# HGRN2 attention with a MetaFormer MLP on one core: chunk scores from a tree of levels, or as a quotient of scanned gate products

## The chip, the cores and the metric

The kernel runs on one core of a Trainium2 chip. That core has a matrix engine (TensorE, PE in the profile; its weight loads are PEld), three engines for elementwise work (VectorE or DVE, ScalarE or ACT, GpSimd or POOL), and a queue (SyncE or SP) from which all of this kernel's transfers are issued. Each engine works off its own instructions in order and waits on semaphores for the others. Matmuls write into PSUM, which the kernel uses in banks of 128 partitions by 512 fp32 numbers; everything else lies in SBUF. The metric is the device time of one execution in microseconds (us).

## The reference, cut to what matters

There are 4 batches, 8 heads, 768 tokens and 48 channels a head. Everything is fp32, except the two MLP weights, which come as float64.

```python
f = 1.0 / (1.0 + np.exp(-f_logit))                  # gates, per channel
for t in range(S):                                  # S = 768
    state = f[:, :, t, :, None] * state + np.einsum('bhd,bhe->bhde', k[:, :, t], v[:, :, t])
    y[:, :, t] = np.einsum('bhd,bhde->bhe', q[:, :, t], state)
x = y.transpose(0, 2, 1, 3).reshape(B, S, H * D)    # (4, 768, 384)
xn = (x - mean) / np.sqrt(var + 1e-06) * g_ln       # over the 384 channels
out = x + np.maximum(xn @ w_ch1, 0.0) @ w_ch2       # 384 -> 1536 -> 384
```

q, k and v are normal with spread 0.1, f_logit is normal with mean 2 and spread 0.5, so a gate is near 0.88. Written out, the weight of step s in step t is the product of the gates over (s, t], per channel. A chunk of tokens can therefore be done as matmuls: scores between the tokens of the chunk, times v, plus q (with the gates from the chunk's start) times the state that enters the chunk.

## The kernel before, in words

The work is cut into 12 units of 256 tokens of one batch (`units`, L71), three to a batch, as two chunks of 128 tokens. A unit has an attention part (`attention`, L180) and an MLP part (`mlp`, L320). Both are Python generators, and the order of all instructions is that in which the program issues them (`manual_schedule`): the loop at L366 to L379 runs, in turn, one step of the attention of unit n and one step of the MLP of unit n - 1. In round 0 the third partner is the conversion of w1 (`weights`, L129), in round 1 that of w2: each weight comes in six pieces of 768 numbers a partition, and each piece goes through DVE (L153), POOL (L155, L157), DVE (L159, L162), ACT (L164) and DVE (L165, L168), or, for w2, POOL at the end (L171).

Attention puts channels on partitions, two heads at partitions 0 and 64, by transposes through an identity on PE (tr, L192), from which ACT copies q and k (z, L198) and makes the gates by a sigmoid (L196). POOL multiplies gates up to products over blocks of 2 to 128 tokens (L207). The scores of a chunk are then made in levels. The diagonal comes first (pd, L218). Then, for blocks of 2, 4, up to 128 tokens, PE multiplies the first half's k with the second half's q (pl, L239), DVE multiplies q and k up to the next block size (L250) and copies the scores under a mask (L256; ACT at the last level, L253). Each level needs the one before. After seven levels k is transposed back (kp, L269), its product with v is the chunk's part of the state (pn, L292), and scores and carried state give y (py, L278 and L285). DVE advances the state (L301, L303), ACT copies y to x (L316).

The MLP normalizes x with DVE and POOL (L328 to L334), transposes it (xp, L341), and has 36 matmuls of 128 x 128 by 256 tokens (ph, L349) with a relu on ACT after each six (L351), then for each 128 tokens twelve accumulating matmuls by 384 columns (po, L356); DVE adds x (L361) and SP stores. ph, po, xp, tr and kp share four PSUM banks, one each; pd, pl and py share two buffers of two banks.

## Time and profile before

| | us |
|---|---|
| median of three runs (935.0, 940.1, 940.43) | 940.1 |
| the profiled execution: span, first to last instruction | 937.5 |
| PE busy | 811.8 (87%) |
| DVE busy | 367.9 (39%) |
| ACT busy | 136.7 (15%) |
| POOL busy | 86.6 (9%) |
| mean granted TensorE clock | 0.837 |

For the profiled execution nothing beside its span is known; the median lies 2.6 above it. The profile page gives, after busy times, the span in 40 equal slices of 23.4 us; a digit is the busy share in tenths. Then it has the chain of waits: followed back from the last instruction, at each step to what released it. A row of a group of instructions has the line, the engine, the operation, the tile written and the tiles read, the shapes, the count, the busy time, the mean of one in ns, and the idle time before it with what ended it. The granted clock is the share of full speed that PE was allowed. PE's records are pipelined, so the price of a group of matmuls is better read from start to start than from its duration.

### The profile page before, as it was taken

The page shows a single profiled execution, that of the slowest core. Times are in us where ns is not written, and L with a number is a line of the kernel's source. Part 1 is how long each engine was busy: PE and PEld are TensorE (multiplying, and loading weights), DVE is VectorE, ACT ScalarE, POOL GpSimd, SP SyncE. Part 2 cuts the span into 40 slices and gives each one's busy share as a digit, 9 for nine tenths or more (in the row PEclk, how much of TensorE's full clock was granted, in tenths as well). Part 3 has the DMA queues.
Part 4 walks back from the last instruction along what each step waited for, and adds up shares of the span by engine and source line. Part 5 has one row for each costly group of instructions (what it writes and reads, how often), then busy time and mean ns, then how long its engine had stood idle before and what let it go on. Part 6 is the DMA issues. An engine that isn't in the chain of part 4 may idle for free.

```text
span 937.5 us, 13603 instructions
## 1 busy us (share of the span) xinstructions
PE 811.8 (87%) x6056; PEld 651.6 (69%) x6056; DVE 367.9 (39%) x490; ACT 136.7 (15%) x229; POOL 86.6 (9%) x168
## 2 busy tenths in 40 slices
PE   3335567989989989989989989989989989989988
PEld 2335555758868768768768768768868868768765
DVE  1675377325225244135125235135225245245110
ACT  2011211111111111111111111111111111111110
POOL 4210333010010010010010010010010010010000
PEclk8555757897997988898897988897897998979989
DMA  9227120021050050050050050050050050000000
GB/s 190 79 67 135 34 68 34 1 57 29 1 84 2 1 85 1 1 85 1 1 85 1 1 84 1 1 85 1 2 80 5 1 84 1 1 17 1 10 8 17
DMA packets 106250, 33.91 MB, mean 36 GB/s; under 512 B 100816, under 2 KB 103888, under 8 KB 106192
## 3 DMA queue, kind: packets, MB, share of 16 engines
q1 hardware_dynamic: 106192, 33.04, 19.8%
q8 instruction: 48, 0.79, 0.3%
q14 instruction: 10, 0.08, 0.0%
HBM read 28.31 MB, written 4.72 MB: 35 GB/s over the span
## 4 chain that ended last, share of the span: by engine, by line
PE 76%; DVE 13%; ACT 4%; POOL 2%; SPq 2%; issue 1%; DMA 1%; POOLq 0%; ACTq 0%
PE ph L349 23%; PE po L356 21%; PE pl L239 18%; PE py L278 6%; DVE scores L221 3%; PE py L285 2%; DVE z L250 2%; PE xp L341 2%; SPq L89 2%; ACT z L198 2%; DVE scores L256 1%; PE pn L292 1%; DVE z L224 1%; PE pd L218 1%; PE kp L269 1%
## 5 line engine op out<-in xcount | busy, mean ns | idle before, releaser
L239 PE MATMUL pl<-z 48*128 48x64 f32 (+1 forms) x2688 | 204.8, 314 | 98.3 <-DVE z L224 59.9
L239 PEld LDWEIGHTS pl<-z 48*128 48x128 f32 (+1 forms) x2688 | 192.5, 226 | 125.1 <-issue 124.4
L349 PE MATMUL ph<-xt,w 128*128 128x256 f32 x864 | 237.3, 432 | 4.7 <-ACT xt L342 4.7
L349 PEld LDWEIGHTS ph<-xt,w 128*128 128x128 f32 x864 | 181.3, 217 | 37.9 <-ACT xt L342 5.3
L356 PE MATMUL po<-w,h 128*128 128x384 f32 x576 | 205.3, 513 | 0.0
L250 DVE TENSOR_TENSOR z<-z,gates 128x512 f32<-128x512 f32 x168 | 115.1, 727 | 165.0 <-PE pl L239 165.0
L356 PEld LDWEIGHTS po<-w,h 128*128 128x128 f32 x576 | 112.8, 201 | 73.4 <-issue 9.7
L256 DVE COPY_PREDICATED scores<-mask,pl 128x1024 f32<-128x1024 int32 x72 | 118.8, 1650 | 0.0
L207 POOL TENSOR_TENSOR gates<-gates 128x512 f32<-128x512 f32 (+6 forms) x84 | 36.0, 429 | 654.2 <-ACT gates L196 648.6
L351 ACT ACTIVATE h<-ph 128x512 f32<-128x512 f32 x72 | 42.9, 596 | 290.6 <-PE ph L349 290.6
L361 DVE TENSOR_TENSOR o<-x,po 128x384 f32<-128x384 f32 x24 | 13.3, 554 | 165.2 <-PE po L356 165.2
L301 DVE TENSOR_TENSOR state<-state,gates 128x192 f32<-128x192 f32 x16 | 5.7, 358 | 129.2 <-PE py L285 129.2
L278 PE MATMUL py<-v,scores 128*128 128x48 f32 x384 | 53.5, 300 | 0.0
L278 PEld LDWEIGHTS py<-v,scores 128*128 128x128 f32 x384 | 50.8, 214 | 1.1
L221 DVE COPY_PREDICATED scores<-diag,pd 128x512 f32<-128x512 int32 x48 | 30.4, 713 | 23.9 <-PE pd L218 23.9
L316 ACT COPY x<-py 128x768 f32<-128x768 f32 x12 | 9.6, 798 | 148.5 <-PE py L285 148.5
L218 PE MATMUL pd<-z 48*128 48x128 f32 x384 | 24.7, 278 | 5.3 <-ACT z L198 5.3
L196 ACT ACTIVATE gates<-tr 128x512 f32<-128x512 f32 x24 | 13.3, 596 | 106.2 <-PE tr L192 106.2
L218 PEld LDWEIGHTS pd<-z 48*128 48x128 f32 x384 | 22.4, 188 | 8.1 <-ACT z L198 7.9
L342 ACT COPY xt<-xp 128x384 f32<-128x384 f32 x24 | 11.4, 478 | 104.6 <-PE xp L341 104.6
L198 ACT COPY z<-tr 128x512 f32<-128x512 f32 x48 | 25.2, 616 | 2.7 <-PE tr L192 2.7
L285 PEld LDWEIGHTS py<-state,z 48*128 48x128 f32 x320 | 20.4, 195 | 7.4 <-issue 6.8
(55 smaller groups left out, 370.0 us busy)
## 6 DMA issues: line engine op xcount, KB each, us to landing
fraw<-in_f_logit_dram SPq DMA_DIRECT2D x24, 192.0 KB, 3.9
qraw<-in_q_dram SPq DMA_DIRECT2D x24, 192.0 KB, 4.8
kraw<-in_k_dram SPq DMA_DIRECT2D x24, 192.0 KB, 5.2
v<-in_v_dram SPq DMA_DIRECT2D x24, 192.0 KB, 4.9
w1words<-in_moe_w_ch_dram SPq DMA_DIRECT2D x6, 768.0 KB, 4.4
w2words<-in_moe_w_ch_dram SPq DMA_DIRECT2D x6, 768.0 KB, 4.3
out_dram<-o SPq DMA_DIRECT2D x24, 192.0 KB, 1.9
gain<-in_moe_g_ln_dram SPq DMA_DIRECT2D x1, 1.5 KB, 3.9
```

Of the source, the lines that this page charges most:

```text
L198: nc.scalar.copy(out=to, in_=pt)
L207: nc.gpsimd.tensor_tensor(out=prod[size], in0=pv[:, 0], in1=pv[:, 1], op=ALU.mult)
L218: nc.tensor.matmul(pd[:, par, a], lhsT=z[rows, 1, a, c * C:(c + 1) * C], rhs=z[rows, 0, a, c * C:(c + 1) * C], start=True, stop=True)
L221: nc.vector.copy_predicated(out=scv[:, par, c], mask=diag.unsqueeze(1).broadcast_to([P, NP, C]), data=pd[:, par])
L239: nc.tensor.matmul(plv[0:m, par, c, a].rearrange("s (n h) -> s n h", h=half), lhsT=z[rows, 1, a, c * C:c * C + m], rhs=late, start=True, s ...
L250: nc.vector.tensor_tensor(out=zz, in0=zz, op=ALU.mult, in1=pv[:, i].broadcast_to([P, nblk, half]))
L256: nc.vector.copy_predicated(out=sc.rearrange("s i (n two h) -> s two i n h", two=2, h=half)[:, 1], mask=masks[half].rearrange("s (o n h) - ...
L278: nc.tensor.matmul(py[:, par, at:at + D], lhsT=scv[:, par, c, a], rhs=vt[:, c, 2 * a + par], start=c == 0 and a == 0, stop=u == 0 and c == ...
L285: nc.tensor.matmul(py[:, par, at:at + D], lhsT=z[rows, 0, a, c * C:(c + 1) * C], rhs=state[rows, a], start=False, stop=True, skip_group_ch ...
L349: nc.tensor.matmul(ph[:, j], lhsT=w1[:, m, (i + j) * P:(i + j + 1) * P], rhs=xt[:, m], start=m == 0, stop=m == KD - 1)
L351: nc.scalar.activation(out=h[:, i:i + 2], in_=ph, func=AF.Relu)
L356: nc.tensor.matmul(po, lhsT=h[:, i, c * C:(c + 1) * C], rhs=w2[:, i], start=i == 0, stop=i == KF - 1)
```

## The change

Units are now 64 tokens of all four batches (256 tokens as before, 12 units), so that the chunk is 64 tokens and one unit follows another in every batch. The levels are gone. A scan on DVE multiplies the gates backward from each chunk's end (`after`, with a new start at every chunk by a zero in the gates), and k times it is kh. A second scan multiplies forward, started at one over the chunk's whole product (`upto`), and q times it is qh. Then kh times qh is the score in one matmul per batch and head, of which DVE keeps the lower triangle (`causal`). As the state that enters is multiplied by the whole product first (`kept`), qh serves for it too. POOL makes kh and qh. The padding channels of f are filled with 40, so that their gates are 1.

Scores, carried, values and state are four groups of 32 matmuls a unit with at most 64 rows and 64 weight columns, at four places of the array in turn. Transposes and MLP are as before in number and shape.

The order is written by slots: attention of units 0, 1 and 2 first, with w1's conversion (18 steps) cut in between; then for each m the MLP of unit m in 12 slots (six of ph, six of po), with the four stages of attention m + 3 behind slots 0, 1, 6 and 8, and normalization and transposes of unit m + 1 behind slots 9 and 10. During m = 0 three steps of w2's conversion, that is one whole piece, stand behind each slot until w2 is done. The weights of the next piece are fetched one piece ahead. w1's pieces are 256 columns of all three row blocks, so their last product is three instructions.

A quotient can overflow when the gates are small. So the least product of a chunk is kept (`least`), compared with 1e-12 near the end, and read into registers; if it is smaller, the kernel before, in a serial form (`general_path`), computes everything again behind a branch.

```diff
--- before.py
+++ after.py
...
+def general_path(tc, q, k, v, f_logit, w1, w2, ident, out):
...
+    for n in range(len(units)):
+        load(n)
+        for _ in attention(n):
+            pass
+        for _ in mlp(n):
+            pass
...
+    T = 64
+    G = B // 2
+    NP = H // 2
+    GA = G * NP
+    NS = 2 * GA
+    E1 = T + 1
...
+    AHEAD = 3
...
+    def load(n):
+        if n >= NU:
+            return
+        vt = raws.tile([P, G, H, D], FP32, tag="rawv", name=f"v{n}")
+        loaded[n] = [wide_heads[name, n % 2] for name in "fqk"] + [vt]
+        for t, src in zip(loaded[n], (f_logit, q, k, v), strict=True):
+            for b in range(B):
+                nc.sync.dma_start(
+                    out=t[(b % 2) * T:(b % 2 + 1) * T, b // 2, :, 0:D],
+                    in_=src[b, :, n * T:(n + 1) * T, :].rearrange("h p d -> p h d"))
...
+    ends = consts.tile([P, NS, E1], FP32)
+    nc.vector.memset(ends, 0.0)
+    nc.vector.memset(ends[:, :, T:E1], 1.0)
+    starts, gates = [], []
+    for i in range(2):
+        t = consts.tile([P, NS, E1], FP32, name=f"starts{i}")
+        nc.vector.memset(t, 0.0)
+        starts.append(t)
+        t = consts.tile([P, NS * E1 + 1], FP32, name=f"gates{i}")
+        nc.gpsimd.memset(t, 0.0)
+        gates.append(t)
+    least = consts.tile([P, NS], FP32)
...
+        r, w = (rows, PIECE // rows) if scaled else (PIECE // cols, cols)
...
+        fetch(0)
+        for i, (ci, fi) in enumerate(pieces):
+            if i + 1 < len(pieces):
+                fetch(i + 1)
...
+            nc.vector.tensor_scalar(out=scale, in0=high, scalar1=20, scalar2=0x7FF,
+                                    op0=ALU.logical_shift_right, op1=ALU.bitwise_and)
+            nc.gpsimd.tensor_scalar(out=scale, in0=scale, scalar1=float(BIAS + 255),
+                                    scalar2=float(BIAS), op0=ALU.min, op1=ALU.max)
+            nc.gpsimd.tensor_scalar(out=scale, in0=scale, scalar1=float(-BIAS),
+                                    scalar2=float(1 << 23), op0=ALU.add, op1=ALU.mult)
+            yield
+            nc.vector.scalar_tensor_tensor(out=scale, in0=high, scalar=-(1 << 31), in1=scale,
+                                           op0=ALU.bitwise_and, op1=ALU.bitwise_or)
+            nc.vector.tensor_scalar(out=high, in0=high, scalar1=0xFFFFF, scalar2=None,
+                                    op0=ALU.bitwise_and)
+            nc.scalar.activation(out=frac, in_=high, func=AF.Copy, bias=1.0, scale=2.0 ** -20)
+            yield
+            nc.vector.scalar_tensor_tensor(out=frac, in0=low, scalar=2.0 ** -52, in1=frac,
+                                           op0=ALU.mult, op1=ALU.add)
+            if scaled:
+                for c in range(r):
+                    nc.vector.scalar_tensor_tensor(
+                        out=to[:, c], in0=frac[:, c], scalar=gain[:, c:c + 1],
+                        in1=scale[:, c].bitcast(FP32), op0=ALU.mult, op1=ALU.mult)
...
+    def attention(n):
+        fr, qr, kr, vt = loaded.pop(n)
+        gt, st = gates[n % 2], starts[n % 2]
+        gv = gt[:, 0:NS * E1].rearrange("p (s e) -> p s e", e=E1)
...
+        for g in range(G):
+            pt = across(fr, g)
+            nc.scalar.activation(out=gv[:, g * 8:(g + 1) * 8, 1:E1], in_=pt, func=AF.Sigmoid)
...
+        after = work.tile([P, NS, E1], FP32, tag="after", bufs=2, name=f"after{n}")
+        nc.vector.tensor_tensor_scan(
+            out=after.rearrange("p s e -> p (s e)")[:, ::-1], data0=gt[:, NS * E1:0:-1],
+            data1=ends.rearrange("p s e -> p (s e)")[:, ::-1], initial=0.0,
+            op0=ALU.mult, op1=ALU.add)
+        total = work.tile([P, NS], FP32, tag="total", bufs=2, name=f"total{n}")
+        nc.vector.tensor_scalar_max(out=total, in0=after[:, :, 0], scalar1=1e-30)
+        nc.vector.reciprocal(out=st[:, :, 0], in_=total)
+        nc.vector.tensor_tensor(out=least, in0=least, in1=total, op=ALU.min)
+        upto = work.tile([P, NS, E1], FP32, tag="upto", name=f"upto{n}")
+        nc.vector.tensor_tensor_scan(
+            out=upto.rearrange("p s e -> p (s e)"), data0=gt[:, 0:NS * E1],
+            data1=st.rearrange("p s e -> p (s e)"), initial=0.0, op0=ALU.mult, op1=ALU.add)
+        yield
+        for src, dst in ((kr, zk), (qr, zq)):
+            for g in range(G):
+                pt = across(src, g)
+                nc.scalar.copy(out=dst[:, g * 8:(g + 1) * 8], in_=pt)
+        kh = work.tile([P, NS, T], FP32, tag="kh", bufs=2, name=f"kh{n}")
+        qh = work.tile([P, NS, T], FP32, tag="qh", bufs=2, name=f"qh{n}")
+        nc.gpsimd.tensor_tensor(out=kh, in0=zk, in1=after[:, :, 1:E1], op=ALU.mult)
+        nc.gpsimd.tensor_tensor(out=qh, in0=zq, in1=upto[:, :, 1:E1], op=ALU.mult)
+        yield
...
+        if n:
+            kept = work.tile([P, 2, GA, D], FP32, tag="kept", name=f"kept{n}")
+            nc.vector.tensor_tensor(
+                out=kept, in0=state, op=ALU.mult,
+                in1=total.rearrange("p (e b) -> p b e", b=2).unsqueeze(3).broadcast_to(
+                    [P, 2, GA, D]))
+        py = two_banks(f"py{n}")
+        if n:
+            for e, (g, a) in enumerate(pairs):
+                for b in range(2):
+                    for r in range(2):
+                        nc.tensor.matmul(py[half(b), r, e * D:(e + 1) * D],
+                                         lhsT=qh[head_rows(r), 2 * e + b],
+                                         rhs=kept[head_rows(r), b, e], start=e == 0, stop=False,
+                                         skip_group_check=True)
+        ps = two_banks(f"ps{n}").rearrange("s r (e t) -> s r e t", t=T)
+        for e, (g, a) in enumerate(pairs):
+            for b in range(2):
+                for r in range(2):
+                    seg = 2 * e + b
+                    nc.tensor.matmul(ps[half(b), r, e], lhsT=kh[head_rows(r), seg],
+                                     rhs=qh[head_rows(r), seg], start=True, stop=True)
+        sc = work.tile([P, 2, GA, T], FP32, tag="sc", name=f"sc{n}")
+        nc.vector.tensor_tensor(
+            out=sc.rearrange("s r e t -> s (r e) t"), in0=ps.rearrange("s r e t -> s (r e) t"),
+            in1=causal.unsqueeze(1).broadcast_to([P, 2 * GA, T]), op=ALU.mult)
+        kt = work.tile([P, GA, P], FP32, tag="kt", name=f"kt{n}")
+        for g in range(G):
+            pt = one_bank(f"kp{n}").rearrange("p (a c) -> p a c", a=NP)
+            for a in range(NP):
+                e = g * NP + a
+                nc.tensor.transpose(pt[:, a],
+                                    kh[:, 2 * e:2 * e + 2].rearrange("p b t -> p (b t)"), ident)
+            nc.scalar.copy(out=kt[:, g * NP:(g + 1) * NP], in_=pt)
+        yield
...
+        for across_ in range(2):
+            for e, (g, a) in enumerate(pairs):
+                for b in range(2):
+                    r = b ^ across_
+                    nc.tensor.matmul(py[half(b), r, e * D:(e + 1) * D],
+                                     lhsT=sc[half(b), r, e], rhs=vt[half(b), g, 2 * a + r],
+                                     start=n == 0 and e == 0, stop=True,
+                                     skip_group_check=True)
+        if n < NU - 1:
+            pn = two_banks(f"pn{n}")
+            for e, (g, a) in enumerate(pairs):
+                for r in range(2):
+                    for b in range(2):
+                        nc.tensor.matmul(pn[half(r), b, e * D:(e + 1) * D],
+                                         lhsT=kt[half(b), e, half(r)],
+                                         rhs=vt[half(b), g, 2 * a + r], start=True, stop=True)
+            pnv = pn[:, :, 0:GA * D].rearrange("p b (e d) -> p b e d", d=D)
+            if n:
+                nc.vector.tensor_tensor(out=state, in0=kept, in1=pnv, op=ALU.add)
+            else:
+                nc.vector.tensor_copy(out=state, in_=pnv)
+        x = xs.tile([P, G, DM], FP32, tag="x", name=f"x{n}")
+        x_of[n] = x
+        nc.scalar.copy(out=x.rearrange("t g (a r d) -> t r (g a) d", r=2, d=D),
+                       in_=py[:, :, 0:GA * D].rearrange("t r (e d) -> t r e d", d=D))
...
+        xn_of[n] = mv, rstd
+        yield
...
+    def normalize(n):
...
+    def turn(n):
...
+            for b in range(2):
+                nc.sync.dma_start(out=out[2 * g + b, n * T:(n + 1) * T, :], in_=o[half(b)])
...
+    load(1)
+    w1_parts = weights(w1, moe_w_ch1, "w1", True)
+    w2_parts = weights(w2, moe_w_ch2, "w2", False)
...
+    for n in range(AHEAD):
+        stages = attention(n)
+        next(stages)
+        some(w1_parts, 1)
+        next(stages)
+        load(n + 2)
+        some(w1_parts, 2)
+        next(stages)
+        some(w1_parts, 2)
+        next(stages)
+        some(w1_parts, 1)
+    some(w1_parts, 18)
+    normalize(0)
+    turn(0)
+    for m in range(NU):
+        n = m + AHEAD
+        stages = attention(n) if n < NU else iter(())
+        parts = mlp(m)
+        for slot in range(12):
+            next(parts)
+            if m == 0:
+                some(w2_parts, 3)
+            if slot == 0:
+                next(stages, None)
+            elif slot == 1:
+                next(stages, None)
+                load(n + 2)
+            elif slot == 6:
+                next(stages, None)
+            elif slot == 8:
+                next(stages, None)
+            elif slot == 9 and m + 1 < NU:
+                normalize(m + 1)
+            elif slot == 10 and m + 1 < NU:
+                turn(m + 1)
+            if m == NU - 2 and slot == 3:
...
+                nc.vector.tensor_scalar(out=small, in0=least_one, scalar1=LEAST, scalar2=None,
+                                        op0=ALU.is_lt)
+    fast.close()
+    too_small = nc.values_load(small[0:1, 0:1], min_val=0, max_val=1)
+    with tc.If(too_small > 0):
+        with tc.manual_schedule():
+            general_path(tc, q, k, v, f_logit, w1, w2, ident, out)
```

331 lines of the change are left out of this document (210 added, 121 removed).

## The prediction

> **What bounds the kernel now.** I read the page's busy times and slices first, then the chain of waits, then the timeline of one unit, then that of the start.
>
> ```profile
> span 937.5 us, 13603 instructions
> ...
> PE 811.8 (87%) x6056; PEld 651.6 (69%) x6056; DVE 367.9 (39%) x490; ACT 136.7 (15%) x229; POOL 86.6 (9%) x168
> ...
> PE   3335567989989989989989989989989989989988
> ...
> PE 76%; DVE 13%; ACT 4%; POOL 2%; SPq 2%; issue 1%; DMA 1%; POOLq 0%; ACTq 0%
> PE ph L349 23%; PE po L356 21%; PE pl L239 18%; PE py L278 6%; DVE scores L221 3%; PE py L285 2%; DVE z L250 2%; PE xp L341 2%; SPq L89 2%; ACT z L198 2%; DVE scores L256 1%; PE pn L292 1%; DVE z L224 1%; PE pd L218 1%; PE kp L269 1%
> ```
>
> TensorE holds 76% of the chain, and the MLP (ph and po) is only 44 points of it. The level matmuls (pl) are 18 points. So most of the span is PE-bound, except the first seven slices, where PE is 30 to 70% busy. The two must be costed apart. First one unit in the middle, PE alone; the columns are start, duration, engine, line, tile and records (an fp32 matmul leaves two records, a transpose one). The last column is idle time before.
>
> ```profile
> 488.71 3.48 PE L239 MATMUL pl<-z 48*128 48x64 f32 x32 [2.95 <-DVE z L224]
> ...
> 497.28 5.47 PE L349 MATMUL ph<-xt,w 128*128 128x256 f32 x12
> 502.68 2.00 PE L239 MATMUL pl<-z 48*128 48x64 f32 x32
> 504.62 2.86 PE L349 MATMUL ph<-xt,w 128*128 128x256 f32 x12
> 507.40 2.00 PE L239 MATMUL pl<-z 48*128 48x64 f32 x32
> ...
> 525.33 1.04 PE L269 MATMUL kp<-ident,z 128*128 128x128 f32 x8
> 526.21 2.75 PE L356 MATMUL po<-w,h 128*128 128x384 f32 x8
> 528.88 1.14 PE L292 MATMUL pn<-v,kt 128*64 128x48 f32 x32
> 529.95 4.01 PE L278 MATMUL py<-v,scores 128*128 128x48 f32 x32
> 533.76 4.29 PE L356 MATMUL po<-w,h 128*128 128x384 f32 x8
> ...
> 539.01 10.59 PE L356 MATMUL po<-w,h 128*128 128x384 f32 x32
> 549.43 1.04 PE L192 MATMUL tr<-ident,fraw 128*128 128x128 f32 x8
> 550.30 1.04 PE L192 MATMUL tr<-ident,qraw 128*128 128x128 f32 x8
> ```
>
> From start to start these are prices at full clock: six ph matmuls 2.78, sixteen po matmuls 10.42, eight transposes 0.87, sixteen matmuls with 64 weight columns (pn) 1.07 or 67 ns each, sixteen with 128 columns and 48 rows (pl) 1.94 or 121 ns, sixteen with 128 columns and 128 rows (values) about 3.8 or 240 ns. The first pl took 3.48 and the first ph 5.47: the clock was low after 2.95 of idling.
>
> **The middle: a unit of 256 tokens, attention and MLP.** The MLP stays: 6 x 2.78 = 16.7 for ph, 1.5 x 10.42 = 15.6 for po. Transposes stay too: 24 of inputs 2.6, 8 of k 0.9, 6 of xn 0.65. What goes is the seven levels (112 matmuls), the 16 diagonal ones, 16 values, 16 pn, up to 16 carried. In their place stand four groups of 32 small matmuls: carried, scores, values, pn. All have 64 weight columns and 48 or 64 rows. No row shows a matmul limited to one quarter of the array. The pn row (64 columns, 128 rows) gives 67 ns; below lies half of that, if two quarters work at once; above lie 121 and 240. I take 67, the row with the same weight width: 128 x 0.067 = 8.6. Sum 16.7 + 15.6 + 2.6 + 0.9 + 0.65 + 8.6 = 45.1. Before, 60.7 passed between the first pl and the next unit's transposes alone (488.71 to 549.43).
>
> The other engines lie beside this. Their prices:
>
> ```profile
> L256 DVE COPY_PREDICATED scores<-mask,pl 128x1024 f32<-128x1024 int32 x72 | 118.8, 1650 | 0.0
> ...
> L351 ACT ACTIVATE h<-ph 128x512 f32<-128x512 f32 x72 | 42.9, 596 | 290.6 <-PE ph L349 290.6
> ...
> L224 DVE TENSOR_TENSOR z<-z,gates 128x1024 f32<-128x1024 f32 x12 | 14.5, 1206 | 0.0
> ...
> L328 DVE BATCH_NORM_STATS2 stats<-x 128x6 f32<-128x384 f32 x24 | 13.0, 540 | 0.0
> ...
> L171 POOL TENSOR_TENSOR w<-w2frac,w2scale 128x768 f32<-128x768 f32 x6 | 12.5, 2082 | 21.7 <-DVE w2frac L165 21.7
> L207 POOL TENSOR_TENSOR gates<-gates 128x512 f32<-128x512 f32 x12 | 12.5, 1040 | 648.6 <-ACT gates L196 648.6
> ```
>
> On DVE a 1,024-wide tensor operation takes 1.2, so the mask multiply is 1.3, kept and state (768 wide) 0.9 each, two stats with aggregation 1.4 (estimate), xn and o two halves each, about 2.1 together (estimate). The two scans have no row. As a plain two-input operation 1,040 elements would take 1.22; the copy under a mask, 1,024 wide, has 1.65; I take the dearer, 1.7 each. That is 7 beside the scans, and 10 to 11 of 45 with them. [...] POOL's two products kh and qh, 1,024 wide, lie between 2.1 each (the L207 row) and 2.8 (L171); I take 2.4.
>
> Does anything in the slots stall PE? Stage 2 issues its products before ph 2; stage 3 needs them after four more ph and the first of six po slots (2.6 each), some 14 later. Scans (about 4 with the small operations) and products (4.8) fit. xn for the next unit is asked for at slot 9, behind the stats on DVE, and PE turns it after 2.6 of po: it fits with about 2 to spare. The 16 transposes of q and k use four banks in turn, which ACT empties at 0.6 a bank while PE fills one in 0.44; the wait is under 1. The doubled count of input DMAs (16 and not 8 a unit, same bytes) is issued two units early: hidden.
>
> One cost remains: the clock.
>
> ```profile
> 534.00:535.00 1.00, 1.00 (x2) 0.56 (x3) 0.00 (x0) 0.00 (x0) 0.00 (x0) 0.50 0.00 0
> ...
> 23.00:98.00 75.00, 32.66 (x304) 31.08 (x306) 45.55 (x56) 7.51 (x9) 9.94 (x12) 0.52 0.39 91
> ```
>
> At 534 PE is busy 1.00 of the time and yet the granted clock is 0.50: 4.9 of small matmuls (pn and values, 528.88 to 533.76) had just run, and the po after them took 4.29 in place of 2.6. The new unit has two such stretches: carried, scores and kt (5.2), values and pn (4.3). I charge 2.2 a unit, an estimate from that loss of 1.7, for a little more than one drop. [...] So a unit is 45.1 + 2.2 = 47.3.
>
> **The start.** Before, w1 is converted beside attention 0 and the MLP begins at about 125, behind the last turn (123.49). Now three attentions with two w1 pieces each come first. First a piece of the chain of waits (start, duration, what), then the timeline.
>
> ```profile
> 17.48 5.67 DMA w1words<-in_moe_w_ch_dram
> ```
>
> ```profile
> 23.18 0.56 DVE L153 TENSOR_SCALAR w1scale<-w1words 128x768 int32<-128x768 int32 x1 [15.79 <-DMA w1words<-in_moe_w_ch_dram]
> 23.82 0.83 POOL L155 TENSOR_SCALAR w1scale<-w1scale 128x768 int32<-128x768 int32 x1 [11.65 <-DVE w1scale L153]
> 24.73 0.83 POOL L157 TENSOR_SCALAR w1scale<-w1scale 128x768 int32<-128x768 int32 x1
> 25.60 0.96 DVE L159 SCALAR_TENSOR_TENSOR w1scale<-w1words,w1scale 128x768 int32<-128x768 int32 x1 [1.86 <-POOL w1scale L157]
> 26.59 0.56 DVE L162 TENSOR_SCALAR w1words<-w1words 128x768 int32<-128x768 int32 x1
> 27.18 0.89 ACT L164 ACTIVATE w1frac<-w1words 128x768 f32<-128x768 int32 x1 [15.81 <-DVE w1words L162]
> 28.10 0.96 DVE L165 SCALAR_TENSOR_TENSOR w1frac<-w1words,w1frac 128x768 f32<-128x768 uint32 x1 [0.95 <-ACT w1frac L164]
> 29.10 1.02 DVE L168 SCALAR_TENSOR_TENSOR w<-w1frac,gain,w1scale 128x768 f32<-128x768 f32 x1
> ...
> 86.02 1.97 PE L239 MATMUL pl<-z 48*64 48x64 f32 x32 [1.48 <-DVE z L250]
> ...
> 89.38 1.97 PE L269 MATMUL kp<-ident,z 128*128 128x128 f32 x8 [1.39 <-DVE z L250]
> ...
> 91.28 1.91 PE L292 MATMUL pn<-v,kt 128*64 128x48 f32 x32
> ...
> 123.49 0.90 PE L341 MATMUL xp<-ident,xn 128*128 128x128 f32 x3 [0.98 <-DVE xn L334]
> ```
>
> Here each engine waits for the next, and PE runs at half clock (0.52 between 23 and 98), so 32 small matmuls take 3.9 and the k transposes 2.0. Unit 0: the first words land at 23.2 as before (the bytes ahead of them are the same). POOL's two steps of the piece stand ahead of kh and qh on its queue, so these end at 25.6 + 4.8 = 30.4; scores 34.3; kt 36.3 (mask multiply beside it); values 40.2; pn 44.0; state 0.9, stats 1.4, the end of piece 1 on DVE (0.96 and a product now in three parts, 1.1) give 48.4. Units 1 and 2 each: scans and small operations 3.7, first step of a piece 0.56, POOL 1.75, then DVE's rest of the piece and kept 5.6 (longer than kh and qh, 4.8), carried 3.9, scores 3.9, kt 2.0, values 3.9, pn 3.8, state 0.9, stats 1.4, piece 2.1: 33.6. So 48.4 + 67.2 = 115.6; normalize, turn and copy 2.5: the MLP starts at 118, only 7 earlier than before.
>
> **The first MLP unit** carries all of w2, a whole piece in each of slots 0 to 5, with nothing to spread it. DVE's and ACT's queues hold relu, scans and copies behind the waiting conversion. A piece goes round DVE, POOL, DVE, ACT, DVE in 5.7, and POOL's closing product (2.1) stands before the next piece's POOL steps: 7.2 a piece. In order: cold ph and relu 6.0, rest of piece 0 1.9, scans 3.7, piece 1 5.7, its product 2.1, kh and qh 4.8, piece 2 5.2, pieces 3 to 5 21.6, kept 0.9: 52 after the start. PE, waiting there for kept with the first po slot done, then has carried, scores, kt 5.2, the other five po slots 13.0, values and pn 4.3, xn 0.65 and a cold clock at first, 3: 26. Together 78.
>
> **Sum.** 118 + 78 + eight units 378 + three units of MLP alone (16.7 + 15.6 + 0.65 = 33.0) 99 = 673.
>
> ```profile
> 934.05 0.56 DVE L361 TENSOR_TENSOR o<-x,po 128x384 f32<-128x384 f32 x1 [7.19 <-PE po L356]
> ```
>
> After the last matmul 3.4 remain (934.05 to 937.5), and there is now a register load and a branch over the unused path on every engine. No row shows them. They can't gain; the nearest rows are this whole tail, 3.4, and the 5.7 that the first words took to land (17.48); I take 5, with 0 and 15 as bounds. Span 681.5. For the profiled execution only its span is known; the median of the three runs, 940.1, is 2.6 above it. 681.5 + 2.6 = 684.
>
> **Rivals.** *The small matmuls are dearer.* At pl's 121 ns 128 of them cost 6.9 more, nine times: 62, so 746; at values' 240 ns 22 more, nine times: 198, about 882. For it: values with a full-height weight did cost that. Against: pl and pn alternate halves of the array as the new ones do, and pay for weight columns. 0.15, nearly all at the near end.
>
> *The clock stays up* in the start and in the middle. The PE work of the start units (13.7, 17.5 and 17.5 without transposes of inputs) would take half, so 24 go, and 9 x 2.2 = 20 fall away too: 640. For it: ph keeps its 2.78 between stretches of pl of 1.94; against: 0.52 in the start, and 1.97 for a pl at 86 that came behind other PE work. 0.20.
>
> *The scan binds: slower.* Place: DVE in each unit. It has 7 beside two scans of s. Above s = 19 DVE takes over from PE (7 + 2s > 45). Units 1 and 2 of the start have four on their chain, the first MLP unit two. At s = 26 the total is 684 + 6 x 24.3 + 8 x (59 - 47.3) = 923; from 27 on the kernel loses (945), and 30 gives 1,011. A scan is serial and no row bounds it strictly, but every DVE row here is near 1.2 to 1.6 ns an element, and 26 would be 25. 0.02.
>
> *It doesn't do what it says: the general path runs as well.* It decides at a product of 64 gates below 1e-12. With logits around 2 of spread 0.5 the smallest product of the reference's inputs is 8.2e-6. If it ran, it would do the work of the kernel before without its overlap, so at least 940 more: over 1,620. 0.01.
>
> **Numbers.** The forecast 0.62, with a range of its own of 655 to 720 (the start and w2 each off by 10, the tail, the clock charge from 0 to 4 a unit). To hold 8 in 10 the range takes in the warm clock and the near end of dear matmuls: 635 to 760. A measurement of this kernel can tell about 1% from no change. Faster by over 1%: 0.62 + 0.15 + 0.20 less 0.01 for the far end of dear matmuls = 0.96; within 1%: 0.01; slower: 0.02 + 0.01 = 0.03.
>
> **What would show it.** First ph near 118, with DVE and POOL waits between; first po's end near 196; then a period of 47 with PE above 95% busy; 32 small matmuls in 2.1; granted clock falling to 0.50 behind the small stretches; MLP-only units of 33; some 8 after the last o. Wrong would be: a PE idle over 3 in each slot cycle (a stall I missed), small matmuls at 3.9 or more at full clock, DVE above half busy in the middle (the scan), or a tail over 20.

## The result and the profile after

The changed kernel takes 619.45 us (median; 618.69 to 619.94) beside 938.2 us (935.0 to 940.43) for the kernel before on the same chip: a ratio of 0.661, 95% interval 0.658 to 0.664. The forecast was 684 us with a range of 635 to 760. The sign was right; the size was missed by 65 us, and the time lies 16 us below the range. The profiled execution took 619.75 us, 618.0 of it span.

The page of the profile after: span, busy times, the two rows of forty slices for TensorE, and the shares of the chain of waits by engine.

```profile
span 618.0 us, 10918 instructions
...
PE 506.4 (82%) x4841; PEld 393.3 (64%) x4841; DVE 207.9 (34%) x265; ACT 123.2 (20%) x217; POOL 126.8 (21%) x95
...
PE   3061615647099999999999999999999999999995
...
PEclk9556666679579999999999999999999999999999
...
PE 74%; DVE 12%; POOL 5%; SPq 3%; ACT 2%; issue 2%; DMA 1%; ACTq 0%
```

TensorE still carries 74% of the chain, but its row now has two halves: eleven slices in which it is mostly idle, and then 9 in every slice but the last, with the granted clock at 9 from the thirteenth on. Before, the same row alternated 8 and 9.

The same trace cut into the stages that the prediction added up: the start up to the first ph, the first MLP unit, the eight units with attention, the three without. The columns are stretch, length, busy time (count) of PE, PEld, DVE, ACT and POOL, granted clock, DMA share, GB/s.

```profile
0.00:115.20 115.20, 38.88 (x807) 34.93 (x807) 67.76 (x86) 22.53 (x36) 35.90 (x43) 0.68 0.61 124
115.20:193.90 78.70, 49.88 (x414) 38.35 (x415) 29.37 (x38) 14.27 (x23) 28.68 (x21) 0.75 0.26 63
193.90:516.90 323.00, 323.00 (x3250) 250.59 (x3249) 104.86 (x127) 73.95 (x136) 62.17 (x32) 1.00 0.21 40
516.90:611.50 94.60, 94.60 (x374) 69.40 (x372) 5.39 (x13) 12.47 (x22) 0.00 (x0) 1.00 0.06 14
```

| stage | predicted | measured | difference |
|---|---|---|---|
| start, to the first ph | 118 | 115.2 | -3 |
| first MLP unit (w2) | 78 | 78.7 | +1 |
| eight units | 378 | 323.0 | -55 |
| three units of MLP alone | 99 | 94.6 | -4 |
| tail after the last product | 8.4 | 6.5 | -2 |
| outside the span | 2.6 | 1.75 | -1 |

So 55 of the 65 us lie in the third row of that view. PE was busy for 323.00 of 323.00 us there at a granted clock of 1.00: nothing stalled and no clock was lost. The units were simply shorter than their sum, 40.4 each and not 47.3. One of them, PE alone, in the columns of the prediction's second fence:

```profile
193.93 2.75 PE L640 MATMUL ph<-xt,w 128*128 128x256 f32 x12
196.52 1.04 PE L504 MATMUL tr<-ident,fraw 128*128 128x128 f32 x8
...
214.77 1.15 PE L551 MATMUL py<-kept,qh 48*64 48x48 f32 x64
215.74 1.13 PE L561 MATMUL ps<-qh,kh 48*64 48x64 f32 x64
216.80 1.09 PE L572 MATMUL kp<-ident,kh 128*128 128x128 f32 x8
217.73 5.33 PE L647 MATMUL po<-w,h 128*128 128x384 f32 x16
222.98 2.00 PE L581 MATMUL py<-v,sc 64*64 64x48 f32 x61
...
224.87 1.12 PE L590 MATMUL pn<-v,kt 64*64 64x48 f32 x62
225.91 5.43 PE L647 MATMUL po<-w,h 128*128 128x384 f32 x16
...
234.42 2.75 PE L640 MATMUL ph<-xt,w 128*128 128x256 f32 x12
```

From start to start, 32 carried matmuls take 0.97 us (30 ns each), 32 scores 1.06 (33 ns), 32 values 1.89 (59 ns), 32 pn 1.04 (33 ns): 4.96 a unit where the sum had 8.6. The values cost most. Unlike what the description of the change says, they do not visit four places of the array in turn: they alternate between two places on one diagonal, then between the two on the other. And six ph take 2.59 (193.93 to 196.52), not 2.78.

The start came out near the forecast for reasons of which two were wrong. First the timeline of DVE and POOL there, then that of PE (the last line belongs to the first MLP unit):

```profile
28.66 0.56 DVE L457 TENSOR_SCALAR w1scale<-w1words 128x768 int32<-128x768 int32 x1 [14.80 <-DMA w1words<-in_moe_w_ch_dram]
...
31.01 2.16 POOL L534 TENSOR_TENSOR kh<-zk,after 128x1024 f32<-128x1024 f32 x1
31.08 2.90 DVE L464 SCALAR_TENSOR_TENSOR w1scale<-w1words,w1scale 128x768 int32<-128x768 int32 x1 [1.86 <-POOL w1scale L461]
33.13 2.88 POOL L535 TENSOR_TENSOR qh<-zq,upto 128x1024 f32<-128x1024 f32 x1
34.02 2.40 DVE L467 TENSOR_SCALAR w1words<-w1words 128x768 int32<-128x768 int32 x1
```

```profile
67.39 1.96 PE L551 MATMUL py<-kept,qh 48*64 48x48 f32 x64 [18.78 <-DVE kept L541]
...
75.71 1.09 PE L504 MATMUL tr<-ident,fraw 128*128 128x128 f32 x8
...
98.52 1.96 PE L551 MATMUL py<-kept,qh 48*64 48x48 f32 x64 [18.92 <-DVE kept L541]
...
115.17 5.41 PE L640 MATMUL ph<-xt,w 128*128 128x256 f32 x12 [0.57 <-ACT xt L629]
...
170.72 1.96 PE L551 MATMUL py<-kept,qh 48*64 48x48 f32 x64 [19.68 <-DVE kept L541]
```

The first words are used at 28.66, not 23.18. Two DVE steps of the conversion, 0.96 and 0.56 us before, take 2.90 and 2.40 while POOL computes kh and qh. On the other side the four groups of small matmuls took 8.3 us with the k transposes (67.39 to 75.71), where the sum had 17.5, all at half clock. Carried and scores did run at a granted clock of 0.50, and took 1.7 and 1.9 in place of 3.9 each. Values and pn ran at 1.00 by then, and took 1.9 and 1.1 in place of 3.9 and 3.8.

### The profile page after: what moved, and what is told of

Same layout as the page of the kernel before. It is cut to its first block, busy times and chain, and to the rows that moved or that the text cites. A ratio compares the mean times of both kernels' runs of the same rounds, so it can differ in the third digit from the quotient of the medians.

```text
span 618.0 us, 10918 instructions
## 1 busy us (share of the span) xinstructions
PE 506.4 (82%) x4841; PEld 393.3 (64%) x4841; DVE 207.9 (34%) x265; ACT 123.2 (20%) x217; POOL 126.8 (21%) x95
## 4 chain that ended last, share of the span: by engine, by line
PE 74%; DVE 12%; POOL 5%; SPq 3%; ACT 2%; issue 2%; DMA 1%; ACTq 0%
PE po L647 30%; PE ph L640 29%; PE py L581 3%; PE tr L504 3%; SPq L384 3%; PE py L551 2%; PE ps L561 2%; DVE w1scale L464 2%; PE kp L572 2%; PE pn L590 2%; PE xp L628 1%; DVE w1words L467 1%; POOL w L479 1%; DVE w L475 1%; DVE upto L524 1%
## 5 line engine op out<-in xcount | busy, mean ns | idle before, releaser
L640 PE MATMUL ph<-xt,w 128*128 128x256 f32 x864 | 197.2, 387 | 9.7 <-ACT zk L531 9.1
L534 POOL TENSOR_TENSOR kh<-zk,after 128x1024 f32<-128x1024 f32 x12 | 38.8, 3237 | 101.0 <-ACT zk L531 101.0
L514 DVE TENSOR_TENSOR_SCAN after<-gates,ends 128x1040 f32<-128x1040 f32 x12 | 27.9, 2324 | 33.9 <-ACT gates L511 29.6
L561 PE MATMUL ps<-qh,kh 48*64 48x64 f32 x768 | 16.9, 250 | 21.4 <-POOL qh L535 21.4
L535 POOL TENSOR_TENSOR qh<-zq,upto 128x1024 f32<-128x1024 f32 x12 | 33.9, 2826 | 0.0
L561 PEld LDWEIGHTS ps<-qh,kh 48*64 48x64 f32 x768 | 15.7, 164 | 21.8 <-POOL qh L535 21.8
L581 PEld LDWEIGHTS py<-v,sc 64*64 64x64 f32 x768 | 24.9, 142 | 6.6 <-issue 5.1
L524 DVE TENSOR_TENSOR_SCAN upto<-gates,starts 128x1040 f32<-128x1040 f32 x12 | 27.9, 2325 | 0.6
L581 PE MATMUL py<-v,sc 64*64 64x48 f32 x768 | 26.4, 226 | 0.9 <-DVE sc L564 0.9
L541 DVE TENSOR_TENSOR kept<-state,total 128x768 f32<-128x768 f32 x11 | 25.8, 2346 | 0.0
```

Of the source, the lines that this page charges most:

```text
L514: nc.vector.tensor_tensor_scan(out=after.rearrange("p s e -> p (s e)")[:, ::-1], data0=gt[:, NS * E1:0:-1], data1=ends.rearrange("p s e -> ...
L524: nc.vector.tensor_tensor_scan(out=upto.rearrange("p s e -> p (s e)"), data0=gt[:, 0:NS * E1], data1=st.rearrange("p s e -> p (s e)"), ini ...
L534: nc.gpsimd.tensor_tensor(out=kh, in0=zk, in1=after[:, :, 1:E1], op=ALU.mult)
L535: nc.gpsimd.tensor_tensor(out=qh, in0=zq, in1=upto[:, :, 1:E1], op=ALU.mult)
L541: nc.vector.tensor_tensor(out=kept, in0=state, op=ALU.mult, in1=total.rearrange("p (e b) -> p b e", b=2).unsqueeze(3).broadcast_to([P, 2, ...
L561: nc.tensor.matmul(ps[half(b), r, e], lhsT=kh[head_rows(r), seg], rhs=qh[head_rows(r), seg], start=True, stop=True)
```

## The experiments

**Why 30 ns.** The matmuls of the old kernel with 64 weight columns took 67 ns, the new ones 30 to 59. The old kernel even had some of the new size, 48 rows by 64 columns: the last level of pl, which the prediction shows at half clock (86.02). At full clock, PE timeline of the kernel before:

```profile
521.56 1.15 PE L239 MATMUL pl<-z 48*64 48x64 f32 x32
```

Sixteen of them take 1.08 us (the next ph starts at 522.64), 67 ns each. Their loop alternates between two row halves at the same columns, so it visits two places of the array and not four. Theory Q: four places of the array (two row halves by two column halves) work at once when the loops visit them in turn, and the order of issue decides the price. Theory S: the smaller shape alone is cheaper. The first kernel keeps every matmul and changes only the order: the carried ones go through a whole quarter before the next, the scores alternate between column halves only.

```diff
-            for e, (g, a) in enumerate(pairs):
+            for r in range(2):
                 for b in range(2):
-                    for r in range(2):
+                    for e, (g, a) in enumerate(pairs):
                         nc.tensor.matmul(py[half(b), r, e * D:(e + 1) * D], ...
...
-        for e, (g, a) in enumerate(pairs):
-            for b in range(2):
-                for r in range(2):
+        for r in range(2):
+            for e, (g, a) in enumerate(pairs):
+                for b in range(2):
                     nc.tensor.matmul(ps[half(b), r, e], ...
```

> In the changed kernel 32 carried matmuls take 0.97 us and 32 score matmuls 1.06 at full clock, where 2.1 each was forecast. Here the carried ones are issued a whole quarter of the array at a time (eight in a row on the same rows and columns), and the scores alternate between the two column halves only, on the same row half. Theory Q (matmuls on different quarters run at once; the order decides): carried 4 us or more per 32 (120 ns each or above), scores 2.1 (67 ns, the price of two places in turn). Then the small stretch grows from 3.0 to about 7 us, the granted clock falls below 1.00 in the middle, as it did in the kernel before behind 4.9 us, and a unit goes from 40.5 to 46 to 48: total 670 to 690. Theory S (a matmul of 48 or 64 rows and 64 columns is cheap by its shape, whatever the order): 1.0 for both, clock 1.00, total 619.

It took 672.82 us (one run). Two units of its PE timeline, the first undisturbed, the second with a fall of the clock:

```profile
277.71 3.18 PE L551 MATMUL py<-kept,qh 48*64 48x48 f32 x61
...
280.85 1.74 PE L561 MATMUL ps<-qh,kh 48*64 48x64 f32 x59
282.51 1.09 PE L572 MATMUL kp<-ident,kh 128*128 128x128 f32 x8
...
417.77 1.97 PE L572 MATMUL kp<-ident,kh 128*128 128x128 f32 x8
419.53 7.01 PE L647 MATMUL po<-w,h 128*128 128x384 f32 x16
```

The carried group takes 3.0 us (277.71 to about 280.7), 94 ns each; the scores about 1.75, 54 ns each. Shapes and counts are the same, so theory S falls. The second kernel swaps the roles: carried alternate between row halves, scores go a whole quarter at a time.

```diff
-            for e, (g, a) in enumerate(pairs):
-                for b in range(2):
+            for b in range(2):
+                for e, (g, a) in enumerate(pairs):
                     for r in range(2):
                         nc.tensor.matmul(py[half(b), r, e * D:(e + 1) * D], ...
...
-        for e, (g, a) in enumerate(pairs):
+        for r in range(2):
             for b in range(2):
-                for r in range(2):
+                for e, (g, a) in enumerate(pairs):
                     nc.tensor.matmul(ps[half(b), r, e], ...
```

> The other way round: carried alternate between the two row halves only, on the same column half; scores are issued a whole quarter at a time. Theory Q: carried 2.1 us per 32 (as the values, which also use two places in turn, take 1.8 to 1.9), scores 4 or more, a unit of 46 to 48 with a clock below 1.00 in places, total 670 to 690. If only different row halves run at once, carried stays at 1.0 here and the column-only scores of the other run were dear. Theory S: 1.0 for both, total 619.

It took 661.67 us (one run). Its PE timeline:

```profile
275.93 1.71 PE L551 MATMUL py<-kept,qh 48*64 48x48 f32 x58
...
277.65 3.18 PE L561 MATMUL ps<-qh,kh 48*64 48x64 f32 x61
280.76 1.09 PE L572 MATMUL kp<-ident,kh 128*128 128x128 f32 x8
```

Carried 1.6 us (50 ns), scores 3.15 (98 ns): the prices went with the order, not with the group. One quarter at a time costs 94 to 98 ns, two places in turn 50 to 54 (59 for the values, which alternate on the diagonal of the array), four in turn 30 to 33. Theory Q holds in this: the order decides the price. That places visited in turn work partly at once is my reading of these prices; whether it is the multiplying or the loading of weights that overlaps, these runs don't separate, nor why two places cost 67 in the kernel before. The sizes that I gave the theory for one and two places were too high, and the time stayed below the 670 to 690 that I expected here.

**The clock.** I had charged 2.2 us a unit for falls of the clock behind small matmuls; the changed kernel has none in its eight units (granted clock 1.00). In the first kernel of this section the clock fell in five of the eight units (0.97 on average from 194 to 540; the second quoted unit is one: k transposes 1.97 instead of 1.09, po 7.01 instead of 5.33), in the second in one (0.99), though their uninterrupted stretches of carried, scores and k transposes are equally long, 5.7 and 5.8 us. Is it the length (theory L), or that work at one place at a time counts for little (theory A)? Two kernels change units 4 to 11 alone: one issues each score four times in the order of four places, the other sends only the carried ones a quarter at a time.

```diff
-        for e, (g, a) in enumerate(pairs):
+        for e, (g, a) in enumerate(pairs * (4 if n > 3 else 1)):
+            e %= GA
             for b in range(2):
                 for r in range(2):
                     seg = 2 * e + b
```

> In units 4 to 11 each score matmul is issued four times over (the same result is written four times), the order four places in turn kept. The uninterrupted small matmuls ahead of the po groups are then carried 1.0, scores 4.2 and k transposes 0.9, 6.1 us, longer than the 5.7 of the whole-quarter kernel in which the clock fell in five of eight units. Theory L (the length of such a stretch lets the clock fall): granted clock below 1.00 in at least three of the units, units of 43.7 us with 1.5 to 4 more where it falls, 650 to 665 us in all. Theory A (not the length but how much of the array works at once decides: one quarter at a time counts as little work): granted clock 1.00 through all units, units of 43.7, 619.5 + 8 x 3.2 = 645 us.

```diff
+            order = [(e, b, r) for e in range(GA) for b in range(2) for r in range(2)]
+            if n > 3:
+                order.sort(key=lambda t: (t[2], t[1], t[0]))
-            for e, (g, a) in enumerate(pairs):
-                for b in range(2):
-                    for r in range(2):
+                for e, b, r in order:
```

> In units 4 to 11 only the carried matmuls go a whole quarter at a time; the scores keep their four places in turn. Stretch: carried 3.0, scores 1.05, k transposes 0.9, together 5.0 us. Theory L: 5.0 lies between the 3.0 of the changed kernel (no drop) and 5.7 (five of eight), near the 5.6 with one drop in eight: no drop or one, so 619.5 + 8 x 2.0 = 635 to 638 us. Theory A: the 3.0 at one place alone are what lets the clock fall, as in the kernel with 5.7: drops in several units, the fall seen right behind the carried matmuls, 640 to 650 us.

They took 658.79 and 636.98 us (one run each). PE timeline of the kernel with the fourfold scores, a usual unit and the one in which the clock fell:

```profile
260.38 1.15 PE L551 MATMUL py<-kept,qh 48*64 48x48 f32 x64
261.35 2.04 PE L562 MATMUL ps<-qh,kh 48*64 48x64 f32 x123
264.40 2.09 PE L562 MATMUL ps<-qh,kh 48*64 48x64 f32 x128 [1.01 <-issue]
267.86 0.34 PE L562 MATMUL ps<-qh,kh 48*64 48x64 f32 x5 [1.36 <-issue]
...
448.38 1.97 PE L573 MATMUL kp<-ident,kh 128*128 128x128 f32 x8
```

The eight units of the kernel with carried alone changed, in one window:

```profile
193.90:531.00 337.10, 337.10 (x3235) 265.81 (x3234) 104.75 (x127) 73.08 (x134) 62.11 (x32) 1.00 0.20 39
```

In the kernel with carried alone changed the granted clock stays at 1.00, with 3.0 us at one place in each unit: theory A's falls behind the carried group did not come, and the time is the one that theory L gave. With the fourfold scores the stretch from carried to po is 6.9 to 8.7 us long, and the clock fell in one unit of eight (0.96 from 410 to 454, 1.00 in the other windows), where it is 10.0: theory L's three did not come either. That kernel took 14 us more than A's 645, mostly because PE paused once or twice in the repeated group, 12.6 us in all eight units (1.0 and 1.4 in the quoted one), waiting for nothing that the profile shows; so its stretch wasn't uninterrupted, it tests L less cleanly than meant, and it is by luck that 658.79 lies in L's 650 to 665. The one unit in which its clock fell is also the one with the longest pauses (1.1 and 1.6).

The kernel before shows the same without any experiment. Its stretch of pn and values at 528.88, behind which the prediction saw the clock fall, comes again in other units; one of them, PE timeline:

```profile
741.93 3.77 PE L278 MATMUL py<-v,scores 128*128 128x48 f32 x32
745.54 2.81 PE L356 MATMUL po<-w,h 128*128 128x384 f32 x8
```

Here the same matmuls run for 4.7 us (740.86 to 745.54), and the po behind them takes 2.81 and not 4.29: the clock stays (1.00). Of the three stretches of this kind (317.98, 528.88 and 740.86) one lost the clock; of the eight that also hold carried matmuls (5.8 us where nothing is lost) five did (0.73 to 0.78 in the 9 or 10 us from the values on, 1.00 in the three others). What is left is a list: of eight units, none fell with stretches of 3.0 us (the changed kernel) and 5.2, one with 5.8, five with 5.7, one with 10.0 broken by pauses. So neither the length nor the places alone decide. The cause stays open.

**The first MLP unit.** Theory W: the conversion of w2 holds it at 78.7. The kernel leaves out the loading and conversion of w2 and fills it with a constant.

```diff
-    w2_parts = weights(w2, moe_w_ch2, "w2", False)
+    w2_parts = iter(())
+    nc.vector.memset(w2, 0.01)
```

> Leaves out the conversion and the loads of w2: the tile is filled with a constant, so the output is not the reference's. Theory W (the first MLP unit takes 79 us because six conversion pieces are issued in its slots 0 to 5 and hold DVE, POOL and with them ACT and the kept state): the first unit falls to 41 to 46, total 580 to 586. Theory C (it is long because attention of unit 3 and a cold clock make it so): it stays above 60, total above 600.

It took 583.7 us (one run). First ph of the first unit and of the second, PE timeline:

```profile
115.00 5.22 PE L640 MATMUL ph<-xt,w 128*128 128x256 f32 x12 [0.57 <-ACT xt L629]
...
157.95 2.75 PE L640 MATMUL ph<-xt,w 128*128 128x256 f32 x12
```

The unit takes 43.0, so 35.7 of its 78.7 us are the conversion and the loads of w2; of the two it is the conversion, since in the changed kernel no step of it in this unit waits for a transfer. Theory W holds, and so does the working in the prediction, but its sum came out by two errors of 3 us that cancel: kept was forecast 52 behind the first ph and ended 55.5 behind it in the changed kernel (carried at 170.72, released by kept); PE's rest was forecast at 26 and took 23.

**The tail.** Of 6.5 us behind the last product, how much is the register load and the branch over the general path? The kernel leaves both out.

```diff
-    too_small = nc.values_load(small[0:1, 0:1], min_val=0, max_val=1)
-    with tc.If(too_small > 0):
-        with tc.manual_schedule():
-            general_path(tc, q, k, v, f_logit, w1, w2, ident, out)
```

> Leaves out the register load, the branch and the general path behind it. 6.5 us pass in the changed kernel from the last add on DVE to the end of the span, 3.4 in the kernel before. If the branch costs the difference: 3.4 here, total 616. If something else lengthened the tail (smaller output transfers, for one): 5 to 6.5, total 618 to 619.

It took 616.37 us (one run); its last add on DVE starts at 609.79 of a span of 614.6, so 4.8 remain (3.4 before the change). The register load and the branch are 1.7 of the 5 that I took. Another 1.4 came with something else of the change, which no run separated; SP's last issues, two in 1.11 us where the kernel before has one in 0.33, may be 0.8 of it. The result lies between the two forecasts.

**The start.** With three attentions ahead, the MLP waits for 115 us, but all of w1 is needed before it too. Theory H: each attention ahead costs start time, and the middle doesn't need them. Theory D: with fewer, the units stall on what attention makes. The kernels change `AHEAD = 3` to 1 and to 2.

> Attention only one unit ahead of the MLP (two attention units less before the first MLP, two more beside MLP units); the four w1 pieces that were spread over those two units follow in a row. In the changed kernel a start unit takes 31 us and an attention beside an MLP 8.7 (40.5 against 31.7). Theory H (the head start costs more than it brings, nothing in the middle needs it): the MLP starts near 75 in place of 115, the two units cost 17 more later, total 595 to 600. Rival D (the distance of three is what keeps PE free of waits): with one unit of distance PE waits for stats and normalization in slots 9 to 11 of each unit, 2 to 5 us, twelve times: total 620 to 660.

> Attention two units ahead. Theory H: the MLP starts near 96, one unit more costs 8.7, total 608 to 611. Rival D: as three units, 619 or a little above, if the start is bound by w1 and not by attention.

AHEAD = 1 took 602.72 us (602.44 to 604.44), ratio 0.645 (0.642 to 0.648); AHEAD = 2 took 611.04, ratio 0.653 (0.650 to 0.656). First ph of the first three units with AHEAD = 1, PE timeline:

```profile
81.93 4.46 PE L640 MATMUL ph<-xt,w 128*128 128x256 f32 x12 [0.57 <-ACT xt L629]
...
159.26 2.75 PE L640 MATMUL ph<-xt,w 128*128 128x256 f32 x12
...
199.74 2.75 PE L640 MATMUL ph<-xt,w 128*128 128x256 f32 x12
```

The MLP starts 33 us earlier (100.59 with two ahead), though later than the 75 forecast; the first unit still takes 77.3, the next 40.5, with no wait of PE in it: H holds, D falls. The total, 3 above the 595 to 600 expected, falls by only 17, because the attentions not done ahead are done in the middle: there are then ten units of 40.5 and one of MLP alone, in place of eight and three, and each exchange costs 9 (40.5 less 31.5).

The other suspect is the stretching of DVE beside POOL. This kernel gives kh and qh to VectorE:

```diff
-        nc.gpsimd.tensor_tensor(out=kh, in0=zk, in1=after[:, :, 1:E1], op=ALU.mult)
-        nc.gpsimd.tensor_tensor(out=qh, in0=zq, in1=upto[:, :, 1:E1], op=ALU.mult)
+        nc.vector.tensor_tensor(out=kh, in0=zk, in1=after[:, :, 1:E1], op=ALU.mult)
+        nc.vector.tensor_tensor(out=qh, in0=zq, in1=upto[:, :, 1:E1], op=ALU.mult)
```

> The two products kh and qh on VectorE in place of GpSimd. In the changed kernel DVE's own two-input operations lengthen beside them: kept 2.35 us on average and 0.95 alone, w1scale L464 2.9 and 0.96 alone. Theory P (DVE waits for POOL's two-input operations, so the products cost DVE about their own time anyway): kh and qh take 1.25 each on DVE, the start gains 3 to 5 us a unit, the MLP starts at 101 to 106, the middle stays at 40.5 a unit, total 605 to 610. Rival: DVE's queue is the chain of the start, so 2.5 more on it a unit lengthen it: total 622 to 627.

It took 610.45 us, ratio 0.653 (0.650 to 0.656). Groups by line and shape, busy time and mean ns; first the changed kernel, then this one:

```profile
L534 POOL TENSOR_TENSOR kh<-zk,after 128x1024 f32<-128x1024 f32 x12 | 38.8, 3237 | 101.0 <-ACT zk L531 101.0
L535 POOL TENSOR_TENSOR qh<-zq,upto 128x1024 f32<-128x1024 f32 x12 | 33.9, 2826 | 0.0
L524 DVE TENSOR_TENSOR_SCAN upto<-gates,starts 128x1040 f32<-128x1040 f32 x12 | 27.9, 2325 | 0.6
...
L541 DVE TENSOR_TENSOR kept<-state,total 128x768 f32<-128x768 f32 x11 | 25.8, 2346 | 0.0
```

```profile
L535 DVE TENSOR_TENSOR qh<-zq,upto 128x1024 f32<-128x1024 f32 x12 | 18.1, 1509 | 0.0
L534 DVE TENSOR_TENSOR kh<-zk,after 128x1024 f32<-128x1024 f32 x12 | 14.5, 1207 | 0.0
L541 DVE TENSOR_TENSOR kept<-state,total 128x768 f32<-128x768 f32 x11 | 10.5, 952 | 0.0
```

With one engine doing all of it, every operation runs at its own price: kept 0.95 instead of 2.35, the pair kh and qh 2.7 instead of 6.1. The MLP starts at 108.83, 6 us earlier, though later than the 101 to 106 forecast; the middle stays at 40.5, since DVE there has time to spare. Theory P holds in its direction, at the slow end. Both edits together, AHEAD = 1 and kh and qh on VectorE:

> Both: one unit ahead, products on VectorE. If H and P both hold the gains add: 585 to 595, the fastest so far. If D holds: above 620.

598.78 us (597.26 to 599.74), ratio 0.640 (0.636 to 0.643); the MLP starts at 79.13. The forecast was missed: with only one attention in the start, only one is left to gain in, so 2.8 of the 6 us came.

The last kernel moves both conversions into the start. It fetches w1's words before the second input, keeps AHEAD = 1 and kh and qh on VectorE, gives the words of w1 and w2 separate buffers, and alternates the steps of their pieces, so that one waits while the other computes:

```diff
-    load(1)
...
-    for n in range(AHEAD):
...
+    stages = attention(0)
+    next(stages)
+    next(stages)
+    some(w1_parts, 1)
+    next(stages)
+    some(w2_parts, 1)
+    some(w1_parts, 1)
+    next(stages)
+    for i in range(17):
         some(w1_parts, 1)
+        some(w2_parts, 1)
+        if i == 6:
+            load(1)
+        if i == 12:
+            load(2)
```

> A start built from the findings: attention one unit ahead, products on VectorE, the first w1 words fetched ahead of the second input unit, and both weights converted before the first MLP, their steps in turn, so that DVE works on one piece while the other waits for POOL or ACT. A piece alone takes 7.1 us in a row (50.85 to 57.96 in the run with one unit ahead); DVE's own part of it is 4.3 for w1 and 3.1 for w2. Theory W+H: the start is 44 us of DVE for twelve pieces and 9 for attention, first words near 17, so the MLP starts at 75 to 85, the first MLP unit takes 41 to 44 (it took 43 without w2), then 40.5 a unit: total 565 to 580. Rival L (loads: 9.4 MB of weights and 1.6 to 4.7 MB of inputs at 186 GB/s need 60 to 76 us, and the two w's now share it): the MLP starts at 95 or later, total 585 or above.

580.09 us (579.6 to 580.38), ratio 0.618 (0.615 to 0.622), the fastest of all: 39 less than the changed kernel, at the upper end of the 565 to 580 forecast. Its PE timeline:

```profile
93.91 5.45 PE L640 MATMUL ph<-xt,w 128*128 128x256 f32 x12 [0.57 <-ACT xt L629]
...
137.09 2.75 PE L640 MATMUL ph<-xt,w 128*128 128x256 f32 x12
```

The first words are used at 17.57, 11 earlier, and the first MLP unit takes 43.2 like the one without w2. But the MLP starts at 93.91, not at 75 to 85. A pair of pieces takes 11.5 us (the first step of w1's pieces stands at 42.19, 53.65, 65.14 and 76.60 on DVE), and DVE's first step waits for a DMA only at the first two pieces. So the start comes near the rival's 95 without the rival's cause: what remains is the chain of the conversion itself, and it was not shortened further here. Part of it is the stretching of DVE beside POOL once more: POOL still makes the last product of each piece of w2 (L479), and beside it L464 on DVE takes 2.55 where its own work is 0.96 (at 45.18, for one). That comes five times, 8 us in all, about what the start lies above its forecast; no run moved that product.

## Why the prediction was right and wrong

- **What bounds the middle: right.** PE alone decides; no slot stalled it, the four banks and xn had enough time, and DVE was busy 13.1 of 40.4 us a unit (104.86 over eight), where I had 10 to 11 of 45.
- **The small matmuls: wrong, the step that failed.** "I take 67, the row with the same weight width: 128 x 0.067 = 8.6." They took 4.96 (30, 33, 59 and 33 ns): 3.7 too much, eight times: 29 us in the middle. In the start the same price, doubled for half clock, put 17.5 into each unit, in place of 8.3; part of that difference is the clock, which was back at 1.00 for values and pn. "No row shows a matmul limited to one quarter of the array" was a misreading: the last level of pl is one, at 67 ns, and what should have been asked of it and of pn is how many places their loops visit in turn. It is two, and the change visits four. I had named the bound ("below lies half of that, if two quarters work at once") and then left it out of the rivals and of the range, which priced only dearer matmuls. Half of 67 would have taken 4.3 off nine units, 39 us in all, and put 645 into the range's lower part; with the clock's 20 it is 625. The bound was what came, 30 to 33 ns, in three groups of four: the experiments showed that one place alone costs 95 ns and four in turn a third of it.
- **The clock charge: wrong.** 2.2 a unit, 18 us over eight, against 0 measured. PE had no idle gap there, busy 323.00 of 323.00 us, and the clock stayed at 1.00. The row at 534 was no error, as the falls in the reordered kernel show, with PE busy 346.00 of 346.00 us at a clock of 0.97. But it was one row of eleven like stretches, of which five kept the clock, the same matmuls at 740.86 among them, and I made it a price for every unit. The new stretches, 3.0 and 2.9 us, are also shorter than the old one of 4.9; at my price for the small matmuls they would have been 5.2 and 4.3. That the first error made the second is not shown: 5.2 us were harmless in the kernel with carried alone changed, and why the clock falls stays open.
- **ph: a term slightly off.** 2.78 was read between stretches of pl; without them six ph take 2.59. That is 1.1 a unit, 9 us in the middle and 3.4 in the three units of MLP alone.
- **The start: right in sum, by errors that cancel.** Carried of unit 1 was due at 60.0 and came at 67.39. The words were 5.5 late behind the doubled number of input transfers (issued at 23.25 and not at 17.48; four input transfers take SP's queue 2.67), which I had called hidden because their bytes are the same; cheaper matmuls in unit 0 gave most of that back, and unit 1's scans began 1.9 late. Then the scans took 1.4 more, and DVE's two steps were stretched by 3.8. Unit 1 to unit 2 was 31.1 for 33.6: 9 less in the matmuls, 7 more elsewhere (3.8 in the stretched steps, 1.4 in the scans). From carried of unit 2 to the first ph 16.7 for 24.4, again 9 less in the matmuls.
- **The scan:** 2.32 us each, where I took 1.7. That is 2.2 ns an element, 1.9 times the 1.22 us at which I had put a plain two-input operation of that length. In the middle it costs nothing, since DVE isn't the bound.
- **w2 and the tail:** 78.7 for 78, by two errors of 3 that cancel; 6.5 for 8.4.
- **The rivals.** "The clock stays up" came true for the middle, at 0.20, and not for the start, which ran at 0.68. Dear small matmuls, the scan as a bound and the general path did not come. No rival said that the small matmuls are cheaper. The range's lower end already held a clock that stays up, so this is why it missed: with the 39 us of cheaper matmuls it would have held 619.

## What to carry to other kernels

Small matmuls whose operands fill a quarter of TensorE's array should be issued so that successive ones go to different quarters: for the same instructions the order alone was worth a factor of three here (94 to 98 ns against 30 to 33). A term for which the profile has no row gets both of its bounds in the range, the cheap one too, and a loss that was seen once (the clock) is carried over only after the same stretch has been looked up elsewhere in the trace. When the middle is bound by one engine without a gap, what the other engines can still give lies outside it, mostly in the start: here three moves in it were worth another 39 us.

## What the hardware showed that was not expected

**DVE's operations take longer beside POOL's.** L464 started at 31.08, 0.07 behind kh on POOL (31.01 to 33.17), and ended at 33.98: 0.81 behind kh's end, where its own work takes 0.96. L467 started at 34.02 and ended at 36.42, 0.41 behind qh's end at 36.01, its own work being 0.56. Each ended behind POOL's operation by a little less than the time that it takes alone. kept, 0.95 with kh and qh on VectorE, takes 2.87 beside POOL in the middle (2.35 on average over all units); at 203.50, for one, it ends at 206.37, 0.83 behind kh's end at 205.54. L464 and kept have two inputs and L467 has one. Why they take longer, no view shows.

**PE pauses in a long run of matmuls at four places.** With 160 of them in a row (the kernel with the fourfold scores, 33 ns each), PE stopped once or twice, for 0.8 to 1.6 us, the first time behind 158 to 274 records, with no releaser in the profile. In the changed kernel, where carried and scores end after 128 records, there is no such pause. Where a unit has two pauses, exactly 128 matmul records lie between them, with 128 weight loads; and from one unit to the next the first pause moves by 29 records, modulo 128, as if the places were fixed in the instruction stream. What PE waits for in the pauses, no view shows and no run separated.

**The clock falls without a gap.** In the first reordered kernel the transposes and products behind 4.8 us of small matmuls take up to twice as long (k transposes 1.97 and not 1.09) though PE is busy 346.00 of 346.00 us; it happened in five of eight like units, and in six of eleven like stretches of the kernel before. So such a loss is not the same in each unit, and one row of it is no price.
